# An expert layer in units of 512 tokens, and three smaller moves, in an attention, FFN and expert kernel

## The chip, the cores and the metric

One Trainium2 chip, one of its cores. The metric is the time of one execution on the device in microseconds (us), the median of several runs. The engines work side by side, each through its own queue in order: TensorE (PE, matmuls; PEld is its weight load), VectorE (DVE), ScalarE (ACT), GpSimd (POOL) and SyncE (SP, which issues most DMAs).

## What is computed

```python
# attention: q, k, v of 4 x 8 heads x 576 x 64; only the 32 largest scores of a row count
scores = scale * np.matmul(q, k.transpose(0, 1, 3, 2))
kth = np.partition(scores, -top_k, axis=-1)[..., -top_k:-top_k + 1]
scores = np.where(scores >= kth, scores, -1000000000.0)
attn = np.exp(scores - scores.max(-1, keepdims=True))
x = (attn / (attn.sum(-1, keepdims=True) + 1e-09)) @ v      # 2304 tokens x 512
# FFN, 512 -> 2048 -> 512
h = x @ w_in
x = (np.maximum(h, 0.0) + alpha * np.minimum(h, 0.0)) @ w_out
# experts: the best of 8, each 512 -> 1024 -> 512
logits = x @ w_gate + modality_bias[modality_id]
e_idx = np.argmax(logits, axis=1)
for e in range(E):
    mask = e_idx == e
    h = np.maximum(x[mask] @ w1[e], 0.0)
    out[mask] = gate_w[mask, None] * (h @ w2[e])            # gate_w: the softmax weight of the chosen expert
```

The FFN's weights `w_in` and `w_out` arrive as 64 bit floats, the rest as 32 bit.

## The kernel before, in words

Products are made exact enough by splitting an operand into a high part and a low part (the rest) and adding three matmuls: high with high, high with low, low with high. Attention and FFN do this in f16, the experts in fp32r.

`phase1` runs attention and FFN in one loop over iterations `s_`. There are 72 iterations with attention, each of which takes two tiles of 128 query rows through the stages of a pipeline: scores of the next pair into `SC` (a PSUM tile named `psS`, four banks), top-k on VectorE, the mask (`mask`: line 518 on ScalarE, line 519 on GpSimd), `expo` (line 522), high and low parts (lines 526 and 530), a DMA that transposes, and the products with v (`av`, line 550), which land in `bankO`. That bank also holds the sums of `total` (line 219) and the gate's logits, ranks and counts, each in its own columns. Work beside this main line hangs on hooks: `at(slot, s, f)` runs `f` in iteration `s` at one of the places early, next, gap, mid, late, in this order within an iteration. Small VectorE and GpSimd operations are put into a list `fill`, which is emitted between the operations of a later top-k, or at once by `flush()`.

Before s = -1 and in the first 17 iterations the FFN's weights are made ready (`all_weights`): 32 pieces of 128x512 are read, summed in squares, scaled, and split by `high` (line 271, ScalarE) and `low` (line 279, VectorE), four pieces per iteration at the end of it (`wstep`); the high parts fall into iterations 5 to 8 and 12 to 15, the low parts each an iteration later. `PD, PN = 0, 1` choose among two ways of splitting, and with these values line 279 does all of them.

The FFN goes by chunks of 256 tokens (`chunk`); the last eight tiles of attention form a chunk in two halves. When a chunk's tokens are there, `start_chunk` puts its preparation `c.pre` on hooks: `norm` in the same iteration, `scale` and `high` in the next, `low` and the transposing DMA of `turn` in the one after; its steps `mm1` (24 matmuls into `psH`, line 629) queue for `XLAT = 4` iterations later, one step per iteration, with `mm2` (line 678) two iterations behind. After a chunk the gate runs on hooks: `gate1`, `logits`, `gate2`, `gate2b`, `gate3` (ranks of the tokens within their expert), `gate3b`, `weight`, `inverse`, `place` (which writes the token's number and its weight into `mapD`, the map of slots).

When attention is over, the remaining FFN steps run alone, and block 0 of the experts (256 tokens of the expert that is fullest by the count before the last chunk) is begun between them (`first_block`, `finish`). `blocks` then works out on VectorE which expert and which slots each further block takes, and `moe_phase` runs nine blocks of 256 tokens: `Block.__init__` reads expert and position into registers and fetches the slots, `gather` fetches the tokens (GpSimd), `load` the weights (eight DMAs of 512 KB), `split` makes high and low parts (lines 1272 and 1273), `turn` transposes the tokens through `psH` and `bankO` (line 1282), `mm` (line 1296) writes `h` into one of two banks of `psS` in turn (`hbank`), `relu` reads it (lines 1303 and 1304), `m2` (line 1315) adds into `Y`, two tiles of `psX`, and `store` evicts and scatters (lines 1321 and 1323). The order of TensorE's work in a block is mm(0), mm(1), m2(0), mm(2), m2(1), mm(3), the next block's turn, m2(2), m2(3). Where the fast way can't be trusted (flags of the top-k, or more blocks than planned), a second, exact pass follows.

Of the kernel before, what the change touches and what calls it, by code (L numbers as in the profile page):

```python
# [28 lines left out]
CAP = NT  # L29
SLOTS = E * CAP + 256  # L30
LOWER = 2.0 ** -76
NBLK = NCH + 1
WSTEP = 4
# [9 lines left out]
WL = 1  # L43
PD, PN = 0, 1
RATE = {1: 1.0, 2: 1.0}
CRED = 1.0
XLAT = 4
REL = 2
# [12 lines left out]
def tile_kernel(ctx, tc, q, k, v, w_in, w_out, alpha, mod_id, w_gate, mod_bias, w1, w2, out, dbg=None, force=False):  # L61
# [97 lines left out]
    def run(exact):  # L159
        with ExitStack() as rs:  # L160
            rc = rs.enter_context(tc.tile_pool(name="rc", bufs=1))
            flags = None if exact else rc.tile([128, 2 * 144 + NFB], BF16, name="flags")
            ohs = rc.tile([128, E], F16, name="ohs")
            G.memset(ohs, 0.0)
            mp = Rec()
            with tc.manual_schedule():
                with ExitStack() as ph:
                    blk, over = phase1(exact, ph, rc, rs, flags, ohs, mp)
                mp.B = rs.enter_context(tc.tile_pool(name="moeB", bufs=1))
                moe_phase(MAXBLK if exact else NBLK, blk, mp, None if exact else lambda: doubts(rc, flags, blk, over))  # L170
            if not exact:
                return nc.values_load(blk[0:1, 32:33], min_val=0, max_val=(2 * 144 + NFB) * 128 + MAXBLK)


    def phase1(exact, ph, rc, rs, flags, ohs, mp):
# [412 lines left out]
        def chunk(ci, xn, rs):  # L588
# [135 lines left out]
            def gate3():  # L724
# [9 lines left out]
                for r in range(R):  # L734
# [10 lines left out]
                eng = few()  # L745
                fill.append(lambda: eng.tensor_tensor(sl, sl, oh, op=ALU.mult))
# [34 lines left out]
            c.gate2b, c.gate3b, c.inverse = gate2b, gate3b, inverse  # L781

            def after(s_):
                if c.k == NCH:
                    return
                if c.k == NCH - 1:
# [5 lines left out]
                    at("mid", s_ + 1, gate3)  # L792
                    at("mid", s_ + 1, gate3b)
                    at("mid", s_ + 1, weight)
                    at("mid", s_ + 1, inverse)
# [106 lines left out]
        def start_chunk(ci, rs, s_):  # L902
# [27 lines left out]
        def first_block(s_):  # L930
# [23 lines left out]
            mp.cx = rc.tile([128, 16], F32, name="cx")  # L954
            mp.blk = rc.tile([128, 33], I32, name="blk")
            V.reduce_max(mx, cp, axis=AX.X)
            V.scalar_tensor_tensor(ge, cp, mx, iota8m, op0=ALU.is_ge, op1=ALU.mult)
# [6 lines left out]
            def prepare():  # L964
                oh0 = mp.oh0
                V.tensor_scalar(mp.less, oh0, -256.0, 255.0, op0=ALU.mult, op1=ALU.add)
                V.tensor_scalar(mp.step, oh0, -256.0, float(CAP), op0=ALU.mult, op1=ALU.add)
                V.scalar_tensor_tensor(mp.step[:, 0:7], oh0[:, 1:8], 256.0, mp.step[:, 0:7], op0=ALU.mult, op1=ALU.add)
                V.tensor_scalar(mp.base, io16[:, :, 0], oh0[:, 0:1], 256.0, op0=ALU.add, op1=ALU.mult)

# [12 lines left out]
        def finish(c):  # L983
# [13 lines left out]
            c.gate3()  # L997
            c.gate3b()
            c.weight()
            c.inverse()  # L1000
# [4 lines left out]
            o.m2(0, (0,))  # L1005
            blk, over = blocks(rc, ohs, mp, state.ffn.tile([128, 2, 256], F32, name="gr", bufs=GR))
            o.m2(0, (1,))
# [139 lines left out]
    def blocks(rc, ohs, mp, le):  # L1147
# [19 lines left out]
        V.tensor_scalar(blk[:, 16:32], cx, float(E * CAP), None, op0=ALU.min)  # L1167
        over = cx[:, 0:1]
        V.tensor_scalar(over, cbi[:, 7:8], float(1 - NBLK), 0.0, op0=ALU.add, op1=ALU.max)
        return blk, over  # L1170
# [14 lines left out]

    def moe_phase(nblk, blk, mp, check):
        def block(i):
# [16 lines left out]
        for i in range(1, nblk):  # L1204
# [7 lines left out]
            for fp in range(4):  # L1212
# [3 lines left out]
                o.relu(fp)  # L1216
                if fp == 0 and i in (2, 4) and check:
                    check = check()
                if fp == 3 and nxt:
# [11 lines left out]
    class Block:  # L1231
# [68 lines left out]
        def relu(self, fp):  # L1300
            h = self.h
            gg = [self.mp.A.tile([128, 2, 256], F32R, name="g" + s_, bufs=2) for s_ in "hl"]
            A.activation(gg[0], h, AF.Relu)  # L1303
# [55 lines left out]
```

## Time and profile before

| | |
|---|---|
| median of 3 runs | 1177.89 us (1176.23 to 1180.07) |
| the profiled execution | 1176.18 us, its span 1174.5 us |
| busy, share of the span | PE 73%, DVE 74%, ACT 66%, POOL 60% |
| expert weights | `w<-in_moe_w_dram` x80, 512.0 KB each |
| chain of waits, by engine | PE 32%, POOL 17%, ACT 16%, DVE 12%, DMA 10% |

The profile is one execution. Its page gives each engine's busy time in 40 equal slices, a chain of work that ended last, followed back from the end, and groups of instructions. A view by windows gives busy times in stretches; a timeline lists instructions with the idle time before them and what ended it.

### The profile page before, as it was taken

The page shows a single profiled execution, that of the slowest core. Times are in us where ns is not written, and L with a number is a line of the kernel's source. Part 1 is how long each engine was busy: PE and PEld are TensorE (multiplying, and loading weights), DVE is VectorE, ACT ScalarE, POOL GpSimd, SP SyncE. Part 2 cuts the span into 40 slices and gives each one's busy share as a digit, 9 for nine tenths or more (in the row PEclk, how much of TensorE's full clock was granted, in tenths as well). Part 3 has the DMA queues.
Part 4 walks back from the last instruction along what each step waited for, and adds up shares of the span by engine and source line. Part 5 has one row for each costly group of instructions (what it writes and reads, how often), then busy time and mean ns, then how long its engine had stood idle before and what let it go on. Part 6 is the DMA issues. An engine that isn't in the chain of part 4 may idle for free.

```text
span 1174.5 us, 22450 instructions
## 1 busy us (share of the span) xinstructions
PE 852.5 (73%) x7484; PEld 628.1 (53%) x7484; DVE 870.5 (74%) x2842; ACT 780.0 (66%) x1288; POOL 701.2 (60%) x1090
## 2 busy tenths in 40 slices
PE   0202221436799989788788779989998899999995
PEld 0001111224466666466455546667666788888885
DVE  5779889788889999999787789992224465556440
ACT  5456696889878887878788878884325365445441
POOL 4175477777988889888789798895322212111200
PEclk9999955658799999989899889999999999999998
DMA  8969976676785676675779678763105497666600
GB/s 247 258 159 214 272 159 159 131 156 155 168 199 131 132 173 120 132 166 112 148 147 202 133 162 162 142 124 52 19 22 176 153 371 246 205 209 199 207 27 21
DMA packets 310488, 187.05 MB, mean 159 GB/s; under 512 B 246545, under 2 KB 279313, under 8 KB 310362
## 3 DMA queue, kind: packets, MB, share of 16 engines
q1 hardware_dynamic: 306586, 175.02, 62.1%
q0 software_dynamic: 3776, 10.51, 2.5%
q8 instruction: 60, 0.98, 0.4%
q14 instruction: 66, 0.54, 0.2%
HBM read 98.20 MB, written 25.94 MB: 106 GB/s over the span
## 4 chain that ended last, share of the span: by engine, by line
PE 32%; POOL 17%; ACT 16%; DVE 12%; DMA 10%; issue 7%; SPq 3%; POOLq 0%; ACTq 0%; DVEq 0%
PE psS L1296 9%; PE psX L1315 8%; PE psX L678 6%; POOL S L519 6%; POOL HL L530 3%; ACT HL L526 3%; PE psS L629 3%; ACT S L522 3%; PE psH L629 3%; DMA rawk<-in_k_dram 2%; DMA PT<-HL 2%; POOL g L665 2%; ACT S L449 2%; ACT u L518 2%; DVE m L469 2%
## 5 line engine op out<-in xcount | busy, mean ns | idle before, releaser
L678 PE MATMUL psX<-Wo,g 128*128 128x512 f16 x864 | 218.1, 403 | 39.9 <-POOL g L665 28.0
L519 POOL TENSOR_TENSOR S<-u,S 128x576 f32<-128x576 bf16 x144 | 188.6, 1331 | 80.5 <-ACT u L518 80.3
L629 PEld LDWEIGHTS <-Wi 128*128 128x128 f16 x1920 | 170.4, 99 | 41.2 <-DVE gr L657 13.2
L530 POOL TENSOR_TENSOR HL<-S,HL 128x512 f16<-128x512 f32 x144 | 167.7, 1165 | 28.6 <-issue 16.6
L445 PE MATMUL psS<-QK 128*128 128x512 f16 (+1 forms) x160 | 64.9, 444 | 154.0 <-DVE B L463 124.0
L629 PE MATMUL psH<-xT,Wi 128*128 128x256 f16 (+1 forms) x1488 | 157.6, 265 | 7.0 <-DVE gr L657 7.0
L522 ACT ACTIVATE S<-S,bc,nb 128x576 f32<-128x576 f32 x144 | 124.3, 864 | 54.5 <-POOL S L519 54.3
L678 PEld LDWEIGHTS <-g 128*128 128x128 f16 x864 | 83.1, 103 | 141.5 <-POOL g L665 36.6
L445 PEld LDWEIGHTS <-QK 128*128 128x128 f16 (+1 forms) x320 | 32.7, 111 | 213.2 <-DVE B L463 80.2
L1323 POOL DMA_INDIRECT out_dram<-o,ids x20 | 19.9, 995 | 164.2 <-ACT o L1321 164.0
L469 DVE MAX8 m<-X 128x8 f32<-128x160 f32 x432 | 117.1, 312 | 0.0
L518 ACT ACTIVATE u<-S,bc 128x576 bf16<-128x576 f32 x144 | 103.1, 764 | 12.4 <-POOL bc L498 12.4
L665 POOL TENSOR_TENSOR g<-gr,g 128x512 f16<-128x512 f32 x72 | 84.0, 1167 | 45.2 <-ACT g L664 42.6
L526 ACT ACTIVATE HL<-S 128x576 f16<-128x576 f32 x144 | 91.4, 680 | 16.1 <-DMA PT<-HL 15.6
L1304 DVE SCALAR_TENSOR_TENSOR gl<-psS,gh 128x512 fp32r<-128x512 f32 x40 | 27.6, 691 | 99.0 <-ACT gh L1303 99.0
L449 ACT ACTIVATE S<-psS 128x576 f32<-128x576 f32 x144 | 84.3, 635 | 17.2 <-PE psS L446 17.0
L1303 ACT ACTIVATE gh<-psS 128x512 fp32r<-128x512 f32 x40 | 23.9, 596 | 107.2 <-PE psS L1296 107.2
L550 PEld LDWEIGHTS <-PT 128*128 128x128 f16 (+1 forms) x2240 | 84.7, 107 | 9.1 <-issue 8.3
L550 PE MATMUL bankO<-VV,PT 128*128 128x66 f16 (+1 forms) x2240 | 88.6, 202 | 0.0
L493 DVE MATCH_REPLACE8 X<-m,X 128x160 f32<-128x160 f32 x288 | 86.6, 308 | 0.0
L466 DVE SCALAR_TENSOR_TENSOR X<-psS,S 128x288 f32<-128x288 f32 (+1 forms) x144 | 80.7, 602 | 2.5
L445 PE MATMUL psS<-K,QK 128*128 128x512 f16 (+1 forms) x160 | 64.8, 441 | 6.2 <-DMA K<-QK 6.2
(233 smaller groups left out, 2177.5 us busy)
## 6 DMA issues: line engine op xcount, KB each, us to landing
w<-in_moe_w_dram SPq DMA_DIRECT2D x80, 512.0 KB
qkD<-QK SPq DMA_DIRECT2D x16, 576.0 KB
QK<-qkD SPq DMA_DIRECT2D x16, 576.0 KB
wraw<-in_moe_w_in_dram SPq DMA_DIRECT2D x16, 512.0 KB
wraw<-in_moe_w_out_dram SPq DMA_DIRECT2D x16, 512.0 KB
vvD<-VV SPq DMA_DIRECT2D x16, 325.0 KB
VV<-vvD SPq DMA_DIRECT2D x16, 325.0 KB
K<-QK SPq DMA_DIRECT2D x32, 144.0 KB
```

The lines of the kernel that those rows point to most:

```text
L445: T.matmul(ps[rows, 0:512], st, K[:, 4 * j:4 * j + 4, :], start=(n_ == 0), stop=(n_ == 1))
L449: A.activation(t.S, SC[:, t.z, :S], AF.Copy, scale=LOWER)
L469: ops.append(lambda: V.max(o, a_))
L518: A.activation(u, t.S, AF.Relu, scale=-BIG, bias=t.cut)
L519: G.tensor_tensor(t.S, u, t.S, op=ALU.subtract)
L522: A.activation(t.S, t.S, AF.Exp, scale=t.c.negc, bias=t.b)
L526: A.activation(t.HL.rearrange("p a b -> p (a b)")[:, 0:S], t.S, AF.Copy)
L530: G.tensor_tensor(f[:, 640:1152], t.S[:, 0:512], f[:, 0:512], op=ALU.subtract)
L550: T.matmul(oo, l, r, start=(n_ == 0), stop=(n_ == len(ops) - 1), skip_group_check=True)
L629: T.matmul(h[:, fb, :], Wi[:, 4 * cc + f0 // 512, wh, f0 % 512:f0 % 512 + 128], c.xT[:, :R, xh_, cc, :], start=(n == 0), stop=(n == 11))
L665: G.tensor_tensor(g[:, 1], r_, g[:, 0], op=ALU.subtract)
L678: T.matmul(c.X2[r], g[:, gh, fb, r * 128:r * 128 + 128], Wo[:, FB * fp + fb, wh, :], start=(fp == 0 and fb == 0 and n == 0), stop=(fp == c ...
```

## The change

Four things are changed.

1. The first FFN chunk has a preparation of its own, `c.pre0`: `norm` as before, and then `scale` (at once, at the head of the iteration), `high`, `low` and `turn` all in the next iteration; its steps queue two iterations after its start instead of four.
2. `PD, PN = 1, 2`: of every two weight pieces the even one is scaled by ScalarE in place, copied to its high part by a second ScalarE pass, and its low part is subtracted by GpSimd. The odd one is as before.
3. `gate2` adds the biases to the logits at once, instead of through `fill`; so does the read of the ranks, which moves from `gate3` to `gate3b`, an iteration later. What `gate3b` did moves to `gate3c`, `inverse` and `place` come one iteration later.
4. Behind block 0 the experts go by `Unit`: up to four units of 512 tokens and one of 256, planned by `units`. `h` lies in `psX`, `Y` in the four banks of `psS`, and block 0's `Y` in two banks of `psS`. Weights are loaded and split once per unit.

```diff
-PD, PN = 0, 1
+PD, PN = 1, 2
-XLAT = 4
+XLAT = 2, 4
...
-                fill.append(lambda: V.tensor_tensor(L, lg.rearrange("p (r e) -> p r e", r=R), bm[:, c0:c0 + R, :], op=ALU.add))
-                fill.append(lambda: V.reduce_max(mx[:, :, 0], L, axis=AX.X))
+                V.tensor_tensor(L, lg.rearrange("p (r e) -> p r e", r=R), bm[:, c0:c0 + R, :], op=ALU.add)
+                V.reduce_max(mx[:, :, 0], L, axis=AX.X)
...
-                fill.append(lambda: V.tensor_tensor(sl, rk.rearrange("p (r e) -> p r e", r=R),
-                                                    ebase[:, None, :].to_broadcast([128, R, 8]), op=ALU.add))
...
             def gate3b():
+                (sl, sf), eng = c.slots, few()
+                V.tensor_tensor(sl, bankO[:, RANKS:RANKS + 8 * R].rearrange("p (r e) -> p r e", r=R),
+                                ebase[:, None, :].to_broadcast([128, R, 8]), op=ALU.add)
+                fill.append(lambda: eng.tensor_tensor(sl, sl, c.oh, op=ALU.mult))
+
+            def gate3c():
...
             c.pre = [("late", 0, norm), ("gap", 1, scale), ("late", 1, high), ("mid", 2, low), ("late", 2, turn)]
+            c.pre0 = [("late", 0, norm), ("early", 1, lambda: (scale(), flush())), ("next", 1, high), ("gap", 1, low), ("mid", 1, turn)]
...
                 at("mid", s_ + GATE[1] + 1, gate3b)
+                at("mid", s_ + GATE[1] + 2, gate3c)
                 at("mid", s_ + GATE[2], weight)
-                at("mid", s_ + GATE[2] + 1, inverse)
+                at("mid", s_ + GATE[2] + 2, inverse)
                 for r in range(R):
-                    at("late", s_ + GATE[2] + 2 + r, lambda r=r: place(r))
+                    at("late", s_ + GATE[2] + 3 + r, lambda r=r: place(r))
...
-            for slot, x, f in c.pre:
+            for slot, x, f in (c.pre if c.k else c.pre0):
                 at(slot, s_ + x, f)
             for fp in range(c.n):
-                fpq.append((s_ + XLAT, c, fp))
+                fpq.append((s_ + XLAT[c.k > 0], c, fp))
...
+    def units_phase(blk, mp, check):
...
+        us = [unit(0)]
+        us[0].load(0)
+        g1 = us[0].gather()
+        l1 = us[0].load(1)
+        tc.add_manual_dep(l1.ins, g1.ins.name, mybir.DependencyInfo(
+            mybir.DependencyClass.Sync, mybir.DependencyReason.DATA), reason="the tokens go first")
+        us[0].load(2)
+        us[0].split(0)
+        us[0].turn((0, 1, 2, 3))
+        us.append(unit(1))
+        us[0].load(3)
+        mp.b0.m2(3)
+        mp.b0.store()
+        for i in range(NUNIT + 1):
+            u = us[i]
+            n = us[i + 1] if i < NUNIT else None
+            for j in range(8):
+                u.mm(j)
+                u.relu(j)
+                if j == 0 and i in (1, 2) and check:
+                    check = check()
+                if j % 2 == 0:
+                    if j < 6:
+                        u.split(j // 2 + 1)
+                    elif n:
+                        n.split(0)
+                    if n:
+                        n.load(j // 2)
+                if j == 1 and n:
+                    n.gather()
+                if j == 7:
+                    if i + 2 <= NUNIT:
+                        us.append(unit(i + 2))
+                    if n:
+                        n.turn((0, 1))
+                if j:
+                    u.m2(j - 1)
+            if n:
+                n.turn((2, 3))
+            u.m2(7)
+            u.store()
...
+        def mm(self, j):
+            h = self.h = psX.tile([128, 512], F32, name="psX")[:, 0:128 * self.R]
+            w1h, w1l = self.wp[j // 2][0]
+            f0 = 128 * (j % 2)
+            xh_, xl_ = [x_[:, :, 0:128 * self.R] for x_ in self.xt]
+            n = 0
+            for w_, x_ in ((w1h, xh_), (w1h, xl_), (w1l, xh_)):
+                for cc in range(NCC):
+                    T.matmul(h, w_[:, cc, f0:f0 + 128], x_[:, cc, :], start=(n == 0), stop=(n == 11))
+                    n += 1
...
+        def m2(self, j):
+            if j == 0:
+                self.Y = [SC[:, r // 2, 512 * (r % 2):512 * (r % 2) + 512] for r in range(self.R)]
+            gg = self.gs.pop(j)
+            w2h, w2l = self.wp[j // 2][1]
+            for r in range(self.R):
+                for n, (g_, w_) in enumerate(((gg[0], w2h), (gg[0], w2l), (gg[1], w2h))):
+                    T.matmul(self.Y[r], g_[:, r * 128:r * 128 + 128], w_[:, j % 2, :],
+                             start=(j == 0 and n == 0), stop=(j == 7 and n == 2))
...
-                self.Y = [psX.tile([128, DM], F32, name="psX") for _ in range(2)]
+                self.Y = [psX.tile([128, DM], F32, name="psX") if self.i else SC[:, r, 512:1024] for r in range(2)]
```

`units` takes the place of `blocks`: from the counts of tokens per expert it works out whole units, and gives the first expert whose rest is at most 256 tokens the small one. `Unit.split`, `turn`, `relu` and `store` do what the block's methods do, `turn` and `store` for four groups of 128 tokens.

## Rows read from the trace of the kernel before

**Rows 1.** The page's busy tenths in 40 slices.
```profile
PE   0202221436799989788788779989998899999995
...
DVE  5779889788889999999787789992224465556440
```
**Rows 2.** Windows: stretch, its length, each engine's busy time (instructions), clock, DMA.
```profile
366.40:391.30 24.90, 24.90 (x261) 17.89 (x255) 24.72 (x104) 20.15 (x34) 20.58 (x31) 1.00 0.70 157
...
972.40:997.50 25.10, 23.69 (x154) 21.50 (x153) 13.83 (x15) 12.39 (x17) 5.45 (x8) 1.00 0.75 234
```
**Rows 3.** The chain of waits in the expert blocks: start us, us, what.
```profile
987.57 2.89 PE psS L1296 x24
...
991.85 3.14 PE psS L1296 x24
...
1006.29 0.44 PE psH L1282 x4
...
1025.76 2.75 PE psX L1315 x12
```
**Rows 4.** Grouped lines, 947 to 1162 us: count | busy us, mean ns | idle before, releaser.
```profile
L1296 PE MATMUL psS<-xth,w0h 128*128 128x256 f32 x272 | 44.5, 286 | 12.1 <-DVE gl L1304 12.1
```
**Rows 5.** Timeline of the experts' start: start us, us, engine, line, instruction, [idle before].
```profile
912.51 0.48 PE L1315 MATMUL psX<-w1h,gh 128*128 128x512 f32 x1
...
913.87 0.67 DVE L1304 SCALAR_TENSOR_TENSOR gl<-psS,gh 128x512 fp32r<-128x512 f32 x1
...
915.05 0.57 DVE L1157 TENSOR_TENSOR cb<-cb 128x8 f32<-128x8 f32 x3
...
920.11 0.35 SPq L1239 DMA_DIRECT2D ids<-mapD  x1
...
924.97 0.97 POOL L1250 DMA_INDIRECT xg<-x2D,ids  x1 [0.30 <-issue]
...
928.83 0.63 PE L1282 MATMUL psH<-ident,xg 128*128 128x128 f32 x4 [1.97 <-DMA xg<-x2D,ids]
...
932.64 0.64 PE L1296 MATMUL psS<-xth,w0h 128*128 128x256 f32 x4
```
**Rows 6.** Timeline of ScalarE at the end: the last eviction, behind the last `m2`.
```profile
1162.45 0.69 ACT L1321 ACTIVATE o<-psX,ids 128x512 f32<-128x512 f32 x1 [0.71 <-PE psX L1315]
```
**Rows 7.** Grouped lines, 135 to 265 us, the iterations with weight splits.
```profile
L519 POOL TENSOR_TENSOR S<-u,S 128x576 f32<-128x576 bf16 x20 | 29.3, 1485 | 32.3 <-ACT u L518 32.3
L530 POOL TENSOR_TENSOR HL<-S,HL 128x512 f16<-128x512 f32 x20 | 23.3, 1166 | 0.0
...
L279 DVE SCALAR_TENSOR_TENSOR Wi<-Wi,wp0s 128x512 f16<-128x512 f32 x12 | 11.8, 1044 | 0.0
```
**Rows 8.** Timelines of VectorE and ScalarE around iteration 12.
```profile
222.75 0.45 DVE L466 SCALAR_TENSOR_TENSOR psS<-psS,S 128x288 f32<-128x288 f32 x1
...
225.15 0.61 ACT L601 ACTIVATE xjunk<-xn 128x512 f16<-128x512 f32 x1
...
241.49 2.74 DVE L279 SCALAR_TENSOR_TENSOR Wo<-Wo,wp1s 128x512 f16<-128x512 f32 x4 [1.67 <-ACT Wo L271]
```
**Rows 9.** The chain of waits in the iterations with weight splits.
```profile
145.18 2.45 ACT Wi L271 x4
...
185.23 4.69 DVE Wi L279 x4
...
240.75 2.54 ACT Wo L271 x4
```
**Rows 10.** Windows of line 629 (`mm1`) alone, at the pause before the fourth chunk.
```profile
477.20:486.30 9.10, 1.88 (x18) 1.44 (x15) 1.00 0.59 122
486.30:495.40 9.10, 0.00 (x0) 0.00 (x0) 1.00 0.47 88
495.40:502.80 7.40, 0.00 (x0) 0.00 (x0) 0.70 1.08 278
```
**Rows 11.** Waits of VectorE, 280 to 790 us: total us, times, longest.
```profile
DVE sl L743 <- PE bankO L550: 6.0, 1, 6.0
DVE tg L760 <- POOL sm L757: 5.6, 1, 5.6
DVE L L710 <- PE bankO L550: 4.1, 1, 4.1
```

More of the change, by code (lines that the diff above doesn't have):

```diff
@@ L29 @@
 CAP = NT
-SLOTS = E * CAP + 256
+SLOTS = E * CAP + 512
 LOWER = 2.0 ** -76
-NBLK = NCH + 1
+NUNIT = 4
 WSTEP = 4
@@ L169, in run @@
                 mp.B = rs.enter_context(tc.tile_pool(name="moeB", bufs=1))
-                moe_phase(MAXBLK if exact else NBLK, blk, mp, None if exact else lambda: doubts(rc, flags, blk, over))
+                if exact:
+                    moe_phase(MAXBLK, blk, mp)
+                else:
+                    units_phase(blk, mp, lambda: doubts(rc, flags, blk, over))
             if not exact:
@@ L793, in after @@
                     at("mid", s_ + 1, gate3b)
+                    at("mid", s_ + 1, gate3c)
                     at("mid", s_ + 1, weight)
@@ L955, in first_block @@
             mp.blk = rc.tile([128, 33], I32, name="blk")
+            mp.at = rc.tile([128, 8], F32, name="at8")
+            mp.part = rc.tile([128, 8], I32, name="part8")
+            mp.some = rc.tile([128, 8], F32, name="some8")
+            mp.few = rc.tile([128, 8], F32, name="few8")
+            mp.ix = rc.tile([128, 1], F32, name="ix8")
+            mp.over = rc.tile([128, 1], F32, name="over")
             V.reduce_max(mx, cp, axis=AX.X)
@@ L965, in prepare @@
                 oh0 = mp.oh0
-                V.tensor_scalar(mp.less, oh0, -256.0, 255.0, op0=ALU.mult, op1=ALU.add)
+                V.tensor_scalar(mp.less, oh0, -256.0, 255.0 if exact else 0.0, op0=ALU.mult, op1=ALU.add)
                 V.tensor_scalar(mp.step, oh0, -256.0, float(CAP), op0=ALU.mult, op1=ALU.add)
                 V.scalar_tensor_tensor(mp.step[:, 0:7], oh0[:, 1:8], 256.0, mp.step[:, 0:7], op0=ALU.mult, op1=ALU.add)
-                V.tensor_scalar(mp.base, io16[:, :, 0], oh0[:, 0:1], 256.0, op0=ALU.add, op1=ALU.mult)
+                if exact:
+                    V.tensor_scalar(mp.base, io16[:, :, 0], oh0[:, 0:1], 256.0, op0=ALU.add, op1=ALU.mult)
+                else:
+                    V.tensor_scalar(mp.base, io16[:, :, 0], 2.0, oh0[:, 0:1], op0=ALU.mult, op1=ALU.add)
+                    V.tensor_scalar(mp.base, mp.base, 256.0, None, op0=ALU.mult)
+                    V.scalar_tensor_tensor(mp.at, oh0, 256.0, ebase, op0=ALU.mult, op1=ALU.add)
             def start():
@@ L998, in finish @@
             c.gate3b()
+            c.gate3c()
             c.weight()
@@ L1005, in finish @@
             o.m2(0, (0,))
-            blk, over = blocks(rc, ohs, mp, state.ffn.tile([128, 2, 256], F32, name="gr", bufs=GR))
+            blk, over = (blocks if exact else units)(rc, ohs, mp, state.ffn.tile([128, 2, 256], F32, name="gr", bufs=GR))
             o.m2(0, (1,))
@@ L1167, in blocks, with units @@
         V.tensor_scalar(blk[:, 16:32], cx, float(E * CAP), None, op0=ALU.min)
-        over = cx[:, 0:1]
-        V.tensor_scalar(over, cbi[:, 7:8], float(1 - NBLK), 0.0, op0=ALU.add, op1=ALU.max)
+        return blk, None
+    def units(rc, ohs, mp, le):
+        le = le[:, 0, 0:8 * NUNIT].rearrange("p (i e) -> p i e", e=8)
+        cp = bankO[:, COUNTS:COUNTS + 8]
+        T.matmul(cp, ones16, ohs, start=True, stop=True)
+        cn, cb, part, some, few, ix, at, over = mp.cn, mp.cb, mp.part, mp.some, mp.few, mp.ix, mp.at, mp.over
+        V.tensor_tensor(cn, cp, mp.less, op=ALU.add)
+        V.tensor_scalar(part, cn, 511, None, op0=ALU.bitwise_and)
+        V.tensor_scalar(cn, cn, 9, None, op0=ALU.arith_shift_right)
+        V.tensor_scalar(some, part, 1.0, None, op0=ALU.is_ge)
+        V.scalar_tensor_tensor(few, part, 256.0, some, op0=ALU.is_le, op1=ALU.mult)
+        V.tensor_tensor(few, few, iota8m, op=ALU.mult)
+        V.tensor_reduce(ix, few, axis=AX.X, op=ALU.min)
+        V.tensor_scalar(few, iota8m, ix, None, op0=ALU.is_equal)
+        V.tensor_tensor(some, some, few, op=ALU.subtract)
+        V.tensor_tensor(cb[0][:, 8:16], cn, some, op=ALU.add)
+        for i, sh in enumerate((1, 2, 4)):
+            V.tensor_tensor(cb[i + 1][:, 8:16], cb[i][:, 8:16], cb[i][:, 8 - sh:16 - sh], op=ALU.add)
+        cbi = cb[3][:, 8:16]
+        V.scalar_tensor_tensor(mp.step, cb[0][:, 8:16], -512.0, mp.step, op0=ALU.mult, op1=ALU.add)
+        full = [128, NUNIT, 8]
+        V.tensor_tensor(le, io16[:, 0:NUNIT].to_broadcast(full), cbi[:, None, :].to_broadcast(full), op=ALU.is_ge)
+        ef, cx, blk = mp.ef[:, 0:NUNIT], mp.cx[:, 0:NUNIT], mp.blk
+        V.reduce_sum(ef, le, axis=AX.X)
+        V.tensor_scalar(blk[:, 0:NUNIT], ef, float(E - 1), None, op0=ALU.min)
+        V.tensor_tensor(le, le, mp.step[:, None, :].to_broadcast(full), op=ALU.mult)
+        V.reduce_sum(cx, le, axis=AX.X)
+        V.tensor_tensor(cx, cx, mp.base[:, 0:NUNIT], op=ALU.add)
+        V.tensor_scalar(blk[:, 16:16 + NUNIT], cx, float(E * CAP), None, op0=ALU.min)
+        V.tensor_scalar(blk[:, NUNIT:NUNIT + 1], ix, 8.0, float(E - 1), op0=ALU.add, op1=ALU.min)
+        V.scalar_tensor_tensor(at, cb[0][:, 8:16], 512.0, at, op0=ALU.mult, op1=ALU.add)
+        V.tensor_tensor(at, at, few, op=ALU.mult)
+        V.reduce_sum(over, at, axis=AX.X)
+        V.tensor_scalar(ix, ix, 0.0, float(E * CAP), op0=ALU.is_ge, op1=ALU.mult)
+        V.tensor_tensor(blk[:, 16 + NUNIT:17 + NUNIT], over, ix, op=ALU.add)
+        V.tensor_scalar(over, cbi[:, 7:8], float(-NUNIT), 0.0, op0=ALU.add, op1=ALU.max)
@@ L1183, in doubts, with unit @@
         return end
-    def moe_phase(nblk, blk, mp, check):
+    def units_phase(blk, mp, check):
+        def unit(i):
+            return Unit(i, 2 if i == NUNIT else 4, blk[0:1, i:i + 1], blk[0:1, 16 + i:17 + i], mp)
+        us = [unit(0)]
[39 more added lines that the diff above has]
+            u.store()
@@ L1187, in block, with moe_phase @@
+    def moe_phase(nblk, blk, mp):
         def block(i):
@@ L1216, in moe_phase @@
                 o.relu(fp)
-                if fp == 0 and i in (2, 4) and check:
-                    check = check()
                 if fp == 3 and nxt:
@@ L1301, in relu @@
             h = self.h
-            gg = [self.mp.A.tile([128, 2, 256], F32R, name="g" + s_, bufs=2) for s_ in "hl"]
+            gg = [self.mp.A.tile([128, 512], F32R, name="g" + s_, bufs=2).rearrange("p (a b) -> p a b", a=2) for s_ in "hl"]
             A.activation(gg[0], h, AF.Relu)
```

67 lines of the change are left out of this document (64 added, 3 removed).

## The prediction

> **What bounds the kernel now.** I read the busy tenths first. They show two regimes [rows 1]: through the first 27 slices VectorE is mostly at 7 to 9, and from slice 28 on it falls to half or less while TensorE stands at 8 to 9. The windows confirm it [rows 2]: in a steady attention stretch of 24.9 us (iterations 25 to 27) TensorE is busy all 24.9 us and VectorE 24.7, so both are full; in one expert block of 25.1 us TensorE has 23.7 and VectorE 13.8. The expert stage therefore belongs to TensorE, and what it costs is read from the chain of its blocks [rows 3]. Per 256 tokens there are four `mm` of 24 matmuls (2.87 to 2.89 us: 120 ns for 256 columns) and four `m2` of 12 (2.75 to 2.77 us: 229 ns for 512 columns). Between the first `mm`, which ends at 990.46, and the second lies a hole of 1.4 us, and the second then takes 3.14 us, 0.27 more. The two groups of four transposes take 2 x 0.44. That is 4 x 2.87 + 4 x 2.75 + 1.4 + 0.27 + 0.9 = 25.1, the period of a block. The holes' total stands in the grouped lines [rows 4]: 12.1 us in front of `mm`, released by the `gl` of line 1304. The second `mm` writes the other bank of `psS`, yet it waits until the first has been read: a write to this tile waits for reads of it anywhere.
>
> All sums are made on the profiled execution (span 1174.5, time 1176.2 us, so 1.7 outside the span); the median of the runs, 1177.9, is 1.7 above it.
>
> **The experts in units of 512.** Nine blocks behind block 0 become four units of 512 tokens and one of 256: the token slots stay 2304. The reference's own routing of its inputs gives two experts 1136 and 1168 tokens; 256 go to block 0, the rest makes two units each, and 112 tokens are the small one, so it just fits.
> A unit does 8 x 12 matmuls in `mm` and 8 x 12 in `m2`, all of 512 columns: 192 x 0.229 = 44.0 us. Sixteen transposes cost 1.9. `h` now lies in two tiles of `psX`, so the hole and its 0.27 go: the second `mm` has its own tile, the third waits for a read that ends during the second. A unit takes 45.9 us against 50.2 for two blocks. Next in line would be the output: `Y` fills all of `psS`, and the next unit's `m2` must wait for four evictions of 0.69 us [rows 6], 2.8 us, but two `mm` (5.5 us) lie in between; if they didn't, it would cost 2.8 per unit. ScalarE and VectorE do 12.4 and 13.8 us per block [rows 2], hence less than 28 per unit: they keep up. Weight loads fall from 80 to 48 of 512 KB; they were hidden, so that is worth nothing. The small unit takes 8 x (12 x 0.120 + 6 x 0.229) = 22.5, and about 0.6 where a weight split stands ahead of its small `relu`. Sum: 3 x 45.9 + 45.0 (its successor has eight transposes) + 23.1 + 1 for restarts = 206.9 us. Before, the same work took from 932.6 [rows 5] to 1162.4 [rows 6], 229.8 us: -22.9.
> The start gives some back [rows 5]. (a) Block 0's `Y` moves from `psX` into `psS`, so its `m2` must now wait for the reads of `h`: the first, at 912.5 now, waits until `gl` ends at 914.5, +2.0; two later ones wait 1.4 each, the hole above. (b) Four gathers instead of two, 1.3 us apart on GpSimd, hold the turning back by 2.6; this runs beside (a). (c) `units` has 21 VectorE operations up to the first position where `blocks` has 14, at 0.2 us, and it follows the late `m2`; the position's DMA waited for the token map until 920.1, so about 1 us shows, within (a). (d) Sixteen transposes through two banks, with an emptying between: about 1.9 more than eight. The first `mm` starts at about 938.2 instead of 932.6: +5.6. If (a) isn't waited for, (b) and part of (d) are left, +2.6 to +4. The second piece's weights, sent behind the fourth gather, have 8 us to arrive. At the very end an eviction of 0.69 us no longer overlaps `m2`: +0.7. The stage: -22.9 + 5.6 + 0.7 = **-16.6**, bounds -20 and -12.
>
> **Half of the low parts.** Of 32 weight pieces the 16 even ones get one more ScalarE pass (0.61, a quarter of the 2.45 us in [rows 9]), and their subtraction goes from VectorE (1.04 us [rows 7]; alone, 2.74 / 4 = 0.69 [rows 8]) to GpSimd (1.17 [rows 7]). They fall into eight iterations, two each: ScalarE +1.2, VectorE -1.4 to -2.1, GpSimd +2.3. In six of the eight the chain runs through ScalarE's four passes (145.2 and 240.8 stand for them), with the mask on ScalarE and then GpSimd behind them: +7.3 if nothing gives. In one it runs through VectorE's four subtractions (185.2, 4.69 us): -2.3 [rows 9]. GpSimd idles ahead of its mask, 32.3 us in ten iterations, for that same ScalarE work [rows 7]; this hides its 2.3, which without cover would cost 18 in all. I take **+4.5**, below 7.3 - 2.3 = 5.0, since not every pass can be last once others grow; bounds -5 (the passes hide, VectorE's saving shows in two or three iterations) and +10 (1.2 in all eight).
> The same four subtractions take 4.69 us beside GpSimd's mask and 2.74 alone. The Trainium skill (SBUF — State Buffer, section "SBUF: two separate sides") says why that may be: the two engines share a port pair, which one of them holds for a whole instruction when VectorE reads two SBUF inputs. The trace agrees so far. By that rule work moved to GpSimd blocks VectorE where they meet, the -2.3 would not come, and the kernel would end 2.3 us later than I say.
>
> **The first chunk two iterations earlier.** The FFN takes one step of 24 matmuls per iteration, and ahead of the fourth chunk it starves: no `mm1` runs from 486.3 to 502.8 [rows 10], two iterations, because that chunk's tokens aren't there. Later chunks keep their distance of four, so the second chunk starts no sooner, a pause opens in iterations 21 and 22, and the FFN's tail is no shorter. Two steps, each about a pair of ScalarE passes, move into iterations that also split weights. The scales now stand at the head of VectorE's iteration 12, which began at 222.75, and the norm that they read only begins on ScalarE at 225.15, two passes long [rows 8]: VectorE's top-k, and behind the scales GpSimd's mask factor, wait 2 to 4 us. In return four ScalarE passes (2.5 us) leave that iteration's end, and the chunk's subtraction moves to where GpSimd idles ahead of the mask. Its transposing DMA passes some loads on SyncE's queue, which nobody needs within an iteration. **-1**, bounds -4 and +4.
>
> **The gate.** In the attention stage VectorE waited 4.1 us for a bank with logits, 6.0 for one with ranks and 5.6 for a GpSimd sum, once each [rows 11]. The two reads now go ahead of later writes to the bank, and the reciprocal one iteration back, so these waits go. Behind the reads now stand TensorE's sums and the products of `av`, until VectorE ends its iteration; the next scores queue behind those. TensorE still has the same queue to run in these iterations, so of 15.7 us I take **-3**, bounds -8 and +2. The token map is written an iteration later, long before it is read.
>
> **The rivals.** *The front gains too*: ScalarE's extra passes hide, VectorE's saving and much of the gate's waits come in full: -16.6 - 5 - 2 - 6 = -30, about 1148. For it: VectorE is full [rows 1]; against it: the chain in rows 9. *The start of the experts gives more back*: the gathers, the weights behind them and the waits on `psS` add up instead of overlapping, some 7 us more: about 1169. *The front loses*: GpSimd's 2.3 and ScalarE's 1.2 us lie on the chain in all eight iterations, +28; with -16.6 and -4 the kernel ends near 1185, slower than before. It decides where more than 2.6 us per iteration show (20.6 / 8). Against it: GpSimd's idle time ahead of its mask. *The units don't fit*: then the exact second pass runs and the time doubles; the counts speak against it. *Gains and losses meet* within 0.3%.
>
> **How the numbers follow.** -16.6 + 4.5 - 1 - 3 = -16.1. On the profiled execution that is 1160.1, on the median 1161.8. Chances: this forecast (1154 to 1167) 0.55, the front gains too 0.17, the start gives more back 0.15, the front loses 0.06, the second pass 0.02, meeting 0.05. The range of 1148 to 1172 takes in the first three. A measurement of this kernel can tell about 0.3% (3.5 us) from no change: faster by more 0.87, within it 0.05, slower 0.08.
>
> **What would show it.** In the new trace `mm` of 12 matmuls should take 2.75 us, a unit 46 us, with no wait for `gl` at its second `mm`; block 0's `m2` should show new waits of 1.4 to 2 us on VectorE, and the first unit should start some 5 us later against the FFN's end. The eight iterations with weight splits should be about half a microsecond longer on average, the early pause should lie in iterations 21 and 22, and the three gate waits should be gone. The prediction is wrong if a unit takes over 48 us, or if the FFN ends more than 8 us earlier or later than now.

## The result, and the profile after

| | median, us | against before (95%) | profiled execution, span |
|---|---|---|---|
| before | 1178.98 | | 1176.18, 1174.5 |
| changed | 1162.2 | 0.985 (0.981 to 0.990) | 1162.94, 1161.2 |

The medians lie 16.8 us apart, the profiled executions 13.2; the forecast was 16.1. I cut both traces at marks that they share: the start of the first exponential of an attention iteration, the first matmul of the FFN's last step, the first and the last matmul of the experts behind block 0.

| stretch, us | before | changed | difference |
|---|---|---|---|
| up to iteration 5 | 136.9 | 136.8 | -0.1 |
| iterations 5 to 16 | 156.6 | 163.7 | +7.1 |
| iterations 17 to 71 | 506.6 | 506.6 | 0.0 |
| FFN alone, up to its last step | 94.9 | 90.1 | -4.8 |
| up to the first unit (nine-block loop) | 37.7 | 43.1 | +5.4 |
| the same nine blocks, four units and a half | 229.8 | 206.9 | -22.9 |
| behind the last matmul | 12.0 | 14.0 | +1.9 |

The experts do what was written: the chain of waits of the changed kernel (start, us, what) shows a row of `mm` (L1353) and `m2` (L1370) with the turning of the next tokens (L1340) inside it; TensorE is busy 206.8 of the 207.0 us from 940.3 on.

```profile
940.47 5.45 PE psX L1353 x24
945.92 2.80 PE psS L1370 x12
...
979.32 0.44 PE psH L1340 x4
...
986.55 5.60 PE psX L1353 x24
```

The hole behind the first `mm` and the slow second one [rows 3] are gone: the first two take 5.45 us together. A unit's period is 986.39 - 940.31 = 46.1 us. At their start block 0's `m2` (L1512), now in `psS`, meets reads of `h` by `gl` (L1501). The timeline of the changed kernel (start, us, engine, line, idle time before and what ended it) has the first two such waits, its chain the third:

```profile
916.82 0.50 PE L1512 MATMUL psS<-w1h,gh 128*128 128x512 f32 x1 [1.94 <-DVE gl L1501]
...
924.25 0.50 PE L1512 MATMUL psS<-w1h,gh 128*128 128x512 f32 x1 [1.41 <-DVE gl L1501]
```
```profile
927.28 2.87 PE psS L1493 x24
930.15 1.41 issue
931.57 3.04 PE psS L1512 x12
```

TensorE stands 1.94, 1.41 and 1.41 us. `units` runs on VectorE ahead of the second of these `gl` (923.50) and adds nothing: the wait is as long as the third, which has no `units` ahead of it.

The FFN's tail is 4.8 us shorter with the same 384 matmuls of `mm1` left in both. 3.5 of it are one step. Before, GpSimd's product `g` (L665) stood behind block 0's gathers, which waited for their ids, and the ids (`mapD` read by SyncE) were fetched only when a write of the map (L764) had landed, for which SyncE waited 3.8 us (timeline of before):

```profile
874.10 0.99 POOL L764 DMA_INDIRECT mapD<-tg,si  x1 [1.75 <-DMA mapD<-tg,si]
...
878.42 0.36 SPq L1239 DMA_DIRECT2D ids<-mapD  x1
...
881.12 1.01 POOL L1250 DMA_INDIRECT xg<-x2D,ids  x1 [4.83 <-DMA ids<-mapD]
882.43 0.96 POOL L1250 DMA_INDIRECT xg<-x2D,ids  x1 [0.30 <-PE psS L629]
...
883.41 1.16 POOL L665 TENSOR_TENSOR g<-gr,g 128x512 f16<-128x512 f32 x1
...
884.62 2.33 PE L678 MATMUL psX<-Wo,g 128*128 128x512 f16 x10 [1.82 <-POOL g L665]
...
888.57 1.16 PE L629 MATMUL psS<-xT,Wi 128*128 128x256 f16 x9 [1.61 <-DVE gr L657]
```

TensorE waits 1.82 and 1.61 us in that step, which begins at 879.59. In the changed kernel it begins at 884.97. The ids are fetched 4.9 us ahead of it instead of 1.2, and now the last map write (L769) waits for them; the gathers start 1.2 us ahead of the step instead of 1.5 behind, and the product is done when TensorE asks for it:

```profile
880.03 0.36 SPq L1436 DMA_DIRECT2D ids<-mapD  x1
...
882.43 1.00 POOL L769 DMA_INDIRECT mapD<-tg,si  x1 [1.14 <-DMA ids<-mapD]
883.74 1.00 POOL L1447 DMA_INDIRECT xg<-x2D,ids  x1 [0.31 <-issue]
...
886.02 1.17 POOL L668 TENSOR_TENSOR g<-gr,g 128x512 f16<-128x512 f32 x1
...
887.59 2.75 PE L681 MATMUL psX<-Wo,g 128*128 128x512 f16 x12
```

Another 1.7 us are the clock (last section), and the last step gives 0.4 back (6.7 us instead of 6.4).

### The profile page after: what moved, and what is told of

It reads as the page before. It is cut to its first block, busy times and chain, and to the rows that moved or that the text cites. A ratio compares the mean times of both kernels' runs of the same rounds, so it can differ in the third digit from the quotient of the medians.

```text
span 1161.2 us, 21475 instructions
## 1 busy us (share of the span) xinstructions
PE 845.0 (73%) x7100; PEld 605.8 (52%) x7100; DVE 816.5 (70%) x2813; ACT 759.2 (65%) x1276; POOL 716.9 (62%) x1106
## 4 chain that ended last, share of the span: by engine, by line
PE 32%; DVE 19%; ACT 16%; POOL 15%; DMA 9%; issue 7%; SPq 2%; ACTq 0%; POOLq 0%; DVEq 0%
PE psS L1370 8%; PE psX L1353 8%; PE psX L681 6%; POOL S L522 4%; PE psS L632 3%; DVE X L496 3%; DVE m L472 3%; POOL HL L533 3%; DMA PT<-HL 3%; ACT HL L529 2%; ACT S L525 2%; POOL qk L414 2%; DVE F L472 2%; PE psH L632 2%; DMA rawk<-in_k_dram 2%
## 5 line engine op out<-in xcount | busy, mean ns | idle before, releaser
L681 PE MATMUL psX<-Wo,g 128*128 128x512 f16 x864 | 220.3, 406 | 38.9 <-POOL g L668 27.8
L632 PEld LDWEIGHTS <-Wi 128*128 128x128 f16 x1920 | 170.1, 99 | 38.5 <-issue 7.0
L533 POOL TENSOR_TENSOR HL<-S,HL 128x512 f16<-128x512 f32 x144 | 167.9, 1166 | 26.9 <-ACT HL L529 15.3
L632 PE MATMUL psH<-xT,Wi 128*128 128x256 f16 (+1 forms) x1488 | 156.9, 264 | 7.1 <-DMA xT<-xhl 5.5
L521 ACT ACTIVATE u<-S,bc 128x576 bf16<-128x576 f32 x144 | 103.1, 764 | 11.9 <-POOL bc L501 11.7
L1360 DVE SCALAR_TENSOR_TENSOR gl<-psX,gh 128x512 fp32r<-128x512 f32 (+1 forms) x40 | 25.4, 636 | 115.5 <-ACT gh L1359 106.8
L553 PE MATMUL bankO<-VV,PT 128*128 128x66 f16 (+1 forms) x2240 | 88.3, 202 | 23.5 <-DVE L L713 13.9
L1359 ACT ACTIVATE gh<-psX 128x512 fp32r<-128x512 f32 (+1 forms) x40 | 22.3, 558 | 109.6 <-PE psX L1353 103.0
L469 DVE SCALAR_TENSOR_TENSOR psS<-psS,S 128x288 f32<-128x288 f32 x72 | 32.9, 457 | 58.6 <-ACT S L452 58.5
```

The source lines that it names most:

```text
L469: ops.append(lambda: V.scalar_tensor_tensor(o, a_, LOWER, b_, op0=ALU.mult, op1=op))
L521: A.activation(u, t.S, AF.Relu, scale=-BIG, bias=t.cut)
L533: G.tensor_tensor(f[:, 640:1152], t.S[:, 0:512], f[:, 0:512], op=ALU.subtract)
L553: T.matmul(oo, l, r, start=(n_ == 0), stop=(n_ == len(ops) - 1), skip_group_check=True)
L632: T.matmul(h[:, fb, :], Wi[:, 4 * cc + f0 // 512, wh, f0 % 512:f0 % 512 + 128], c.xT[:, :R, xh_, cc, :], start=(n == 0), stop=(n == 11))
L681: T.matmul(c.X2[r], g[:, gh, fb, r * 128:r * 128 + 128], Wo[:, FB * fp + fb, wh, :], start=(fp == 0 and fb == 0 and n == 0), stop=(fp == c ...
```

## The experiments

Times against runs of before on the same chip; 0.001 is 1.2 us. The last column is the trace's time for iterations 5 to 16.

| run | what it is | median | ratio (95%) | 5 to 16 |
|---|---|---|---|---|
| e10 | the change once more | 1161.2 | 0.9859 (0.9838 to 0.9880) | 163.7 |
| e4 | experts in units alone | 1163.8 | 0.9870 (0.9842 to 0.9898) | 157.3 |
| e1 | change without low parts | 1153.4 | 0.9793 (0.9770 to 0.9816) | 156.4 |
| e6 | change, subtractions on VectorE | 1155.8 | 0.9815 (0.9791 to 0.9839) | 160.9 |
| e7 | its ScalarE pass given to VectorE | 1159.4 | 0.9840 (0.9809 to 0.9870) | 156.6 |
| e2 | change without early first chunk | 1165.8 | 0.9883 (0.9863 to 0.9904) | 165.0 |
| e3 | change without the gate | 1170.3 | 0.9919 (0.9899 to 0.9939) | 163.9 |
| e5 | change, map writes as before | 1164.3 | 0.9887 (0.9867 to 0.9907) | 163.5 |
| e8 | e1, block 0's `h` in `psX` | 1151.5 | 0.9777 (0.9753 to 0.9800) | 155.8 |
| e9 | e8, `m2` inside the turning | 1149.1 | 0.9766 (0.9741 to 0.9792) | 155.3 |
| e11 | e9 without early first chunk | 1151.2 | 0.9776 (0.9753 to 0.9799) | 156.3 |

**The units alone (e4).** Before, with the new expert loop only (the changed kernel with the edits of e1, e2 and e3 together).

> Before with the experts in units and nothing else of the change. Prediction: 16.6 us below before (bounds 12 to 20): about 1162.4, FFN end as before (894.9 us), the first unit's first matmul about 5.6 us later than 932.6, the units 207 us. Reading of the trace: the same parts, 5.4 + 207.7 + 1.2 more behind the last eviction: 15.5 below before, 1163.5. If the units gave more, near 20, the front of the change would have cost the rest (1159). All of the three other parts together are then the changed kernel less this one: 0.5 by the prediction, 2.3 by the trace.

The kernel is 15.3 us below before (12.0 to 18.6). In its trace the first unit begins 44.6 us behind the FFN's last step. The stage's term holds.

**The low parts (e1, e6, e7).**

```diff
-PD, PN = 1, 2          # e1
+PD, PN = 0, 1
-    G.tensor_tensor(dst[w_][:, i, 1], f, dst[w_][:, i, 0], op=ALU.subtract)     # e6
+    V.tensor_tensor(dst[w_][:, i, 1], f, dst[w_][:, i, 0], op=ALU.subtract)
-    A.activation(f32[x], f32[x], AF.Copy, scale=sc[w_])     # e7
+    V.tensor_scalar(f32[x], f32[x], sc[w_], None, op0=ALU.mult)
```

> The changed kernel with the low parts back on VectorE, all else as changed. The trace of the changed kernel is level with that of before at iteration 5, is 7.2 us late at iteration 16 and 7.0 late at the end of the attention; the weight splits lie in these iterations. Prediction's price for the low parts: +4.5 us, so this kernel should stand 4.5 below the changed one, about 1157.7, and iteration 17 should start about 4.5 earlier than 300.5 us, at 296. Reading of the trace, if the low parts alone are the 7 us: about 1155, iteration 17 at 293 to 294. Rival: the first chunk's steps, moved into the same iterations, cost it: iteration 17 still starts near 300 and the time stays at 1162.

> The changed kernel with the 16 low parts subtracted on VectorE; ScalarE keeps the second pass for these pieces. From iteration 5 to iteration 17 the changed kernel takes 163.7 us, the one without the low parts' change 156.4. Theory (ScalarE's two extra passes lie in the path of all eight iterations, 8 x 1.2 = 9.6 less what the ones between give back): 163 to 166 us here as well, time 1160 to 1164. Rival (GpSimd's two subtractions delay its mask, or the port shared with VectorE): 156 to 158 us, time 1153 to 1155. The prediction had both, 7.3 for ScalarE less 2.3 for VectorE's saving: by it the saving is gone here, and it would be 2.3 above the changed kernel.

> The changed kernel with the extra scaling pass on VectorE in place of ScalarE; GpSimd keeps the subtraction. ScalarE then has its four passes per split iteration as before, VectorE two subtractions and two scalings, GpSimd two subtractions. Theory (ScalarE's extra passes are the cost): iteration 5 to 17 takes 154 to 158 us against 163.7, time 1151 to 1155. Rival (GpSimd's subtractions are the cost): 163 us or more, time 1161 and up. Third case: ScalarE waits for VectorE's scaling behind the top-k, 158 to 163 us, time 1155 to 1161.

Without them the kernel is 0.0066 faster than e10, 7.8 us (about 4 to 11), and iterations 5 to 16 take what they took before. Windows of iterations 5 to 8 (columns: stretch, length, then busy time of PE, PEld, DVE, ACT, POOL, clock, DMA) of the changed kernel, e1, e6 and e7, in this order:

```profile
136.80:191.60 54.80, 15.22 (x149) 10.10 (x150) 39.27 (x136) 51.77 (x92) 43.64 (x70) 0.57 0.72 180
```
```profile
134.60:184.80 50.20, 15.16 (x148) 10.02 (x148) 46.70 (x141) 46.71 (x83) 40.21 (x64) 0.62 0.77 189
```
```profile
137.40:192.50 55.10, 15.51 (x149) 10.35 (x150) 45.60 (x144) 51.75 (x91) 38.45 (x65) 0.62 0.72 184
```
```profile
136.10:186.20 50.10, 15.63 (x149) 10.47 (x150) 45.47 (x144) 46.06 (x84) 47.90 (x70) 0.57 0.71 179
```

The length goes with ScalarE's column alone: 51.8 us of work make 55, 46 to 47 make 50, whoever subtracts. ScalarE is nearly full in the four iterations (it idles 3 to 4 us of them): its eight extra passes add 5.1 us of work, and 4.6 show. GpSimd's eight subtractions cost nothing here (e7 against e1). They cost in iteration 9, where GpSimd is full: in the changed kernel, then in e6 (in e7, which has them too, iteration 9 takes 14.1 us),

```profile
191.60:205.50 13.90, 0.39 (x2) 0.30 (x2) 12.62 (x11) 6.73 (x10) 13.90 (x13) 0.50 0.42 86
```
```profile
192.50:204.20 11.70, 0.41 (x2) 0.32 (x2) 11.46 (x11) 6.74 (x10) 11.70 (x11) 0.50 0.44 84
```

2.2 us for the two subtractions that the split of iteration 8 leaves there, and another 0.7 us each in iterations 13 and 15 (12.4 us, in e6 11.7). Iteration 10 gives back: 17.4 us instead of 21.3 (in e1 and in before), because VectorE's weight reads end 0.5 us into it and not 4.4. This is not VectorE's relief: in e6, where VectorE does all the subtractions, it takes 17.4 as well. The longer iterations ahead gave the reads their time. The eight split iterations are 9.5 us longer in the changed kernel than in e1, iteration 9 is 2.4 longer, iteration 10 3.9 shorter, iteration 16 0.7 shorter: together the +7.3 of the table. By the traces the passes alone are 4.5 of it (e6) and the subtractions 2.8; by the times the passes are 2.6 (0.0022) and the subtractions 5.2 (0.0044 against e10), each with some 4 either way, so the division between them is no finer than that. e7's time does not show its shorter front: it missed its 1151 to 1155 and stands 2 us below e10, with 4 either way. Its trace, of its slowest run, is 13.2 us longer than that of e1. Of this 0.2 lie in iterations 5 to 16, 5.1 in iterations 17 to 71, within the scatter of the next part, 5.3 in the FFN's tail and the experts' start, of which the clock (last section) is a part, and 2.7 at the two ends. So that ScalarE's passes are the cost is shown by the traces of these iterations, not by e7's time.

**The gate (e3, e5).**

```diff
-                V.tensor_tensor(L, lg.rearrange(...), bm[:, c0:c0 + R, :], op=ALU.add)     # e3; the other reads likewise
+                fill.append(lambda: V.tensor_tensor(L, lg.rearrange(...), bm[:, c0:c0 + R, :], op=ALU.add))
-                at("mid", s_ + GATE[2] + 2, inverse)               # e3 and e5
+                at("mid", s_ + GATE[2] + 1, inverse)
-                    at("late", s_ + GATE[2] + 3 + r, lambda r=r: place(r))
+                    at("late", s_ + GATE[2] + 2 + r, lambda r=r: place(r))
```

> The changed kernel with the gate's reads, its reciprocal and its map writes where they were before. Prediction: the gate's move is worth 3 us, in the three waits of VectorE inside the attention: 1165, with the iterations around 580 to 660 us some 3 us longer in sum. Reading of the trace: the iterations of the two kernels differ by nothing there; but the last map write now stands behind block 0's gathers' slot numbers, and the gathers no longer hold the relu product on GpSimd for the last but one FFN step. Then the attention keeps its length (0.5 us either way), and the FFN's tail grows by 3.5 us, again to 1165 to 1166 but from another place. Rival: nothing of the tail hangs on the gate: 1162.

> The changed kernel with the reciprocal and the map writes one iteration earlier again, as before; the gate's direct reads stay. The prediction put the later map write at nothing: then 1162. Reading of the traces: with all of the gate undone the FFN's step from its 14th to its 15th group of 24 matmuls in the tail takes 9.0 to 9.3 us, with the gate changed 5.5. If the place of the map writes does this, it takes 9.0 here too, and the time is 1165 to 1166; the rest of the 8 us that undoing the whole gate cost, some 4.5, then belongs to the direct reads. If the direct reads do it, the step stays at 5.5 and the time at 1162.

Without the whole gate 0.0060 is lost, 7.1 us (4 to 10); with the map writes alone moved back 0.0028, 3.3 us (0 to 7). The traces say which: the FFN's step from its 14th to its 15th group of 24 `mm1` takes 9.0 to 9.8 us in before, e3, e4 and e5, and 5.5 to 5.6 in the other nine traces. In e5 the old row is back:

```profile
886.60 1.16 POOL L668 TENSOR_TENSOR g<-gr,g 128x512 f16<-128x512 f32 x1
...
887.82 2.33 PE L681 MATMUL psX<-Wo,g 128*128 128x512 f16 x10 [2.01 <-POOL g L668]
```

So the later map write, which lets block 0's ids leave ahead of a scatter, gives 3.5 to 4.3 us. What the direct reads give inside the attention stays open: iterations 17 to 71 take 506.6, 509.9 and 509.3 us in the three traces without them and 503.6 to 509.6, 506.3 in the mean, in ten with them. That is 2.3 us for them, a third of the scatter.

**The first chunk (e2, e11).** `XLAT = 4, 4`, and `c.pre` for every chunk.

> The changed kernel with the first chunk prepared as before (its steps spread over three iterations, four iterations ahead), all else as changed. Prediction: the move is worth 1 us, so this one should stand at 1163 (bounds 1158 to 1166); the front's iterations 10 to 16 change their lengths among themselves. Rival (the chunk's steps are what makes iterations 9 to 16 late): iteration 17 starts 3 to 7 us earlier than 300.5 and the time falls to 1156 to 1159. Second rival: the FFN's tail after the attention, which is 4.8 us shorter in the changed kernel with the same 384 matmuls left, owes that to this move; then it grows back and the time is 1166 to 1167.

> The kernel of the first of these runs with the first chunk prepared as before (three iterations, four ahead). With the low parts on GpSimd undoing this cost 3.6 us on the chip and 1.3 in the trace between iterations 5 and 17; the prediction gave the move 1 us. If the move is worth 1 to 3.6 us by itself, this kernel stands that much above the first run; if it only paid beside ScalarE's extra passes, there is no difference or a gain.

2.8 us beside the low parts, 1.2 without them, each with some 3 to 3.5 either way; in the traces iterations 5 to 16 are 1.3 and 1.0 us shorter for the move, which is about as well as that stretch repeats. So about 1 us is likely but not shown, and the FFN's tail owes it nothing (e2: 89.7).

**The experts' start (e8, e9), and the change once more (e10).** e8 and e9 leave the low parts on VectorE.

```diff
-                self.h = hbank().rearrange("p (a b) -> p a b", a=2)       # e8 and e9
+                self.h = (psX.tile([128, 512], F32, name="psX") if self.i == 0 and fp else hbank()).rearrange("p (a b) -> p a b", a=2)
-        us[0].turn((0, 1, 2, 3))                                          # e9
+        us[0].turn((0, 1))
         us.append(unit(1))
         us[0].load(3)
         mp.b0.m2(3)
+        us[0].turn((2, 3))
```

> The changed kernel without its low parts (1153.4 us on the chip) in which block 0's h of the second and later steps lies in psX, so that m2 into psS waits for no read of it. The first unit's first matmul stands 43.1 us behind the FFN's last step there, 37.7 in the kernel before. Term (a) of the prediction (waits of m2 for reads on VectorE: 2.0, 1.7 and 1.4 us in the trace of the changed kernel) says that 3 to 5 us go: 38 to 40 us, time 1149 to 1150. If the gathers set the start (their data land about 934 in the trace of the changed kernel, six us ahead of the first matmul, with the turning of 3 us behind), about 2.5 go: 40.5, time 1151. If neither: 43, 1153.

> The kernel with h of block 0 in psX and without the low parts (1151.5 us on the chip), with block 0's last m2 put between the two halves of the first unit's turning. There TensorE waited 1.3, 1.2 and 0.6 us for the gathered tokens, and the m2 behind these holes ran 1.6 us longer, at a granted clock of one half. If the gathers are the limit, the m2 of 2.8 us fills the holes: the first unit's first matmul moves from 41.5 to 38.5 to 40 us behind the FFN's last step, time 1149 to 1150. If the limit is the emptying of the turned tokens on ScalarE and VectorE (0.6 + 0.7 behind the last transposes), it stays at 41 to 41.5 and 1151.5.

> The changed kernel as it is, beside the next one, to read both on one chip. By the first measurement 16.8 us below before, ratio 0.985; by the sum of the single parts as measured (experts 16.2 less, low parts 8.8 more, first chunk 3.6 less, gate 8.1 less) 19 below, 0.984. The stages as in its first trace: 163.7 us from iteration 5 to 17, 43.1 from the FFN's last step to the first unit.

In e8 no `m2` waits for `gl`, yet the first unit comes only 1.6 us sooner, at 41.5. Its timeline names what is late next, the gathered tokens:

```profile
919.99 0.66 PE L1340 MATMUL psH<-ident,xg 128*128 128x128 f32 x4 [1.31 <-DMA xg<-x2D,ids]
...
922.48 0.63 PE L1340 MATMUL psH<-ident,xg 128*128 128x128 f32 x4 [1.18 <-DMA xg<-x2D,ids]
...
923.69 0.71 PE L1340 MATMUL bankO<-ident,xg 128*128 128x128 f32 x4 [0.58 <-DMA xg<-x2D,ids]
```

Behind these holes the granted clock fell to 0.52 (924.0 to 927.2 us, the lower of TensorE's two levels, 1.2 GHz instead of 2.4), and block 0's last `m2` took 1.6 us longer. In e9 this `m2` stands inside the turning: one hole of 1.47 us is left, the clock stays at 1.00, and the first unit starts at 38.9. e9 is the fastest kernel here, 0.0093 below the changed one (e10, same chip): 11 us, of which the low parts are about 8.

## Why the forecast was right, point by point

- **The total** was right within a microsecond on the medians and 2.9 us off on the profiled executions, but two of its terms were off by some 3 to 4 us with opposite signs: that the total came so close is partly luck.
- **Experts in units**: right in mechanism and size. 206.9 us forecast for the units, 206.9 found, where small errors cancel: a unit's period is 46.1 to 46.3 against 45.9, and the 1 us for restarts does not come separately (the forecast's 1.9 for sixteen transposes should be 1.8 by its own 0.44). The start cost +5.4 against +5.6. The three waits of term (a) were put at 2.0, 1.4 and 1.4 and measured 1.94, 1.41 and 1.41; `units` is hidden within them, as term (c) said. That the gathers run beside (a) and set the start if (a) is gone is what e8 shows. Its 41.5 - 37.7 = 3.8 lies in the forecast +2.6 to +4 by luck, for 1.6 of it is the clock, which the forecast left out. The end cost 1.9 instead of 0.7 (1.2 to 2.5 in the other traces with units); why stays open.
- **Low parts**: the sign right, the size not: +7.3 in the trace, 7.8 on the chip, for +4.5. The step that failed is "in six of the eight the chain runs through ScalarE's four passes": the passes cost in all eight, since where VectorE was last ScalarE idled only 0.3 to 1.3 us (iterations 5, 8, 12 and 14 of e1), and the two passes need 1.2. The second failure is "-2.3" for VectorE's saving: in those same iterations VectorE idles 2.5 us and more in the changed kernel, so its relief is worth nothing there. What does come back, 3.9 us in iteration 10, comes in e6 too, without that relief. The third is the cover: GpSimd's idle time ahead of its mask does hide the subtractions in iterations 5 to 8, but not in iteration 9, where the last two of them land (+2.2 against e6), nor wholly in 13 and 15 (+0.7 each).
- **The Trainium skill's rule** (SBUF — State Buffer, section "SBUF: two separate sides") was to take the -2.3 away by locking VectorE out. The saving didn't come there, but not for that reason: the remaining VectorE subtractions in iterations 5 to 8 got shorter, not longer. In iteration 9, where GpSimd is full, the rule may have a part: VectorE's weight reads around it took 15.0 us in the changed kernel, 13.2 in e1 and 13.7 in e6, and one of them waited 1.0 us for a GpSimd subtraction; no run separates this. The next two rows are subtractions of these iterations, twelve in e1 and the six that are left of them in the changed kernel:

```profile
L282 DVE SCALAR_TENSOR_TENSOR Wi<-Wi,wp0s 128x512 f16<-128x512 f32 x12 | 11.8, 1048 | 0.0
```
```profile
L282 DVE SCALAR_TENSOR_TENSOR Wi<-Wi,wp0s 128x512 f16<-128x512 f32 x6 | 4.4, 747 | 4.2 <-ACT Wi L274 4.2
```

- **First chunk**: -1 forecast, about -1 in the traces. The early pause is where it was put: windows of `mm1` (L632) alone over iterations 20 to 22,

```profile
330.20:341.20 11.00, 2.79 (x24) 2.28 (x24) 0.92 0.76 183
341.20:350.10 8.90, 0.00 (x0) 0.00 (x0) 1.00 0.70 188
350.10:357.60 7.50, 1.13 (x6) 0.86 (x7) 0.65 1.07 253
```

- **Gate**: -3 forecast, about -7 on the chip. The three waits of VectorE [rows 11] are gone, and `av` waits for the reads in their place, as written (13.9 us in the page):

```profile
L553 PE MATMUL bankO<-VV,PT 128*128 128x66 f16 (+1 forms) x2240 | 88.3, 202 | 23.5 <-DVE L L713 13.9
```

  But these waits moved and did not go: from 300 to 800 us VectorE waited 37.3 us in all in before and 42.0 in the changed kernel (37 to 45 in all 13 traces). The largest part is the wait for the next scores, in before and in the changed kernel:

```profile
DVE psS L466 <- ACT S L449: 16.9, 13, 3.0
```
```profile
DVE psS L469 <- ACT S L452: 30.6, 14, 5.8
```

  So the -3 is not shown where it was put: iterations 17 to 71 take 506.6 us in both traces. What failed beside it is "the token map is written an iteration later, long before it is read". The last map write isn't read by block 0, but block 0's ids had stood behind it, its gathers behind the ids, and the FFN's product behind the gathers on GpSimd: 3.5 us, a term that the prediction put at nothing.

## What to carry to other kernels

Before adding a pass to one engine to relieve another, look at the idle time of the receiving engine in the very iterations that get the pass: where that is less than the pass's length, nearly all of it is paid (5.1 us of work cost 4.6 here), and the relief of the other engine may not show at all. When an indirect write or read moves in time, follow its engine's queue to the next instruction of another stage behind it. When a wait goes, look where the engine waits next. And when a forecast's total is right, price its parts one by one: here the change without its low parts is 8 us faster than the change.

## What was not expected of the hardware

TensorE's clock falls in some executions behind holes in its work or behind small matmuls, and not in others of nearly the same program. In before the FFN's `mm2` behind the logits' small matmuls took 4.44 us, in the changed kernel 2.75; windows of before around it (granted clock in the third column from the right: 0.57, most of it at the lower level of 1.2 GHz, between two at 1.00, the level of 2.4):

```profile
856.00:860.00 4.00, 3.70 (x32) 3.20 (x30) 1.20 (x4) 2.20 (x4) 1.39 (x2) 1.00 0.18 74
860.00:864.00 4.00, 4.00 (x14) 1.51 (x12) 1.20 (x9) 0.00 (x0) 0.10 (x1) 0.57 0.02 4
864.00:868.00 4.00, 4.00 (x37) 2.92 (x35) 1.16 (x8) 0.70 (x2) 0.55 (x4) 1.00 0.00 0
```

The window at 0.57 cost 1.7 us; the same step is 10.0 us long in before, e3, e5, e7 and e11 and 8.35 in the other eight traces, whichever parts of the change they hold. The experts' start of e10 is 44.7 us where the first trace of the same kernel has 43.1: behind the first wait for `gl` the granted clock of e10 is 0.52 (916 to 919 us), that of the first trace 1.00 (917 to 920). So a single trace can't tell a term below some 2 us in these stretches; the units, which have none, repeat within 0.2 us, and iterations 5 to 16 within about 1 (e1, e8 and e9 hold the same work there).

A gather's issue on GpSimd took 1.85 us while VectorE's weight subtraction of two SBUF inputs ran beside it in e8, and 1.89 at the same place in e9; the one ahead of it took 0.97. The next issue of e8 (920.24), which began 0.15 us ahead of such a subtraction, took 0.95 beside it. From the timeline of e8:

```profile
916.81 0.97 POOL L1305 DMA_INDIRECT xg<-x2D,ids  x1 [0.30 <-issue]
917.87 1.23 DVE L1330 TENSOR_TENSOR w<-raw,w0h 128x1024 fp32r<-128x1024 f32 x1 [0.58 <-ACT w0h L1329]
918.09 1.85 POOL L1305 DMA_INDIRECT xg<-x2D,ids  x1 [0.30 <-ACT w0h L1329]
```

The issue begins inside the subtraction (917.87 to 919.10) and ends 0.84 us behind it, nearly its usual length. The Trainium skill (SBUF — State Buffer, section "SBUF: two separate sides") says that GpSimd can't write the descriptors of its DMAs while VectorE runs an operation in a 2-port mode, and that whichever of the two starts first gets the shared ports for its whole instruction. These rows would fit that, if a subtraction of two SBUF inputs does the same; no run here tests it.
